# A transformer block on one core: down product in four PSUM banks, weights split in three pieces, SyncE in written order, row transposes in three jobs

## The chip, the cores and the metric

The kernel runs on one core of one Trainium2 chip. The metric is the device time of one execution in microseconds (us). A core has a matrix engine (PE, with its weight loads shown apart as PEld), VectorE (DVE), ScalarE (ACT), GpSimd (POOL) and SyncE (SP), which only issues transfers here. Each engine takes its instructions in one order and waits at the first that is not ready.

## The reference, cut to what matters

```python
x = A_x                                            # 2048 x 576, f32; 32 heads of 18
h  = x + attention(layernorm(x), wqkv) @ wo        # full softmax attention
n  = layernorm(h)
h2 = h + (gelu(n @ w_gate) * (n @ w_up)) @ w_down  # 576 -> 4608 -> 576
```

All tensors are f32 in DRAM. The kernel keeps f32 accuracy on a 16-bit matrix engine by splitting operands into a high and a low f16 part and adding three products.

## The kernel before, in words

**Attention.** The 2048 rows are four blocks of 512. Heads go in groups of four, so that there are 32 steps (group, block), each a loop over 16 key tiles `kt`. For each key tile PE makes the scores of four heads into two-bank tiles `pair0`/`pair1`, ACT exponentiates them (L579), and PE weighs the values into a single bank (`weigh`, L583). VectorE meanwhile takes the row maxima for a later step (`max_unit`, L533), one and a half steps ahead, so that in the last step and a half no maxima are left. What else has to be done in that stretch is dealt out by Python generators: `take(side, 2)` and `take(fill, 2)` advance two helpers by two yields per key tile. `out_block` normalises a finished step and sends it by DMA into the transposed store `XT`. `wo_block(b)` is the output projection of block b (8 groups of 14 matmuls of 288 columns, evicted by VectorE at L688). `pair_rows(0)` makes the rows for the first pair of blocks and transposes them by DMA.

**The gated product.** The 576-wide product with gate and up weights uses a seven-product scheme for 2x2 blocks, over pairs of row blocks p = 0, 1 (`pair_rows(p)` makes the seven row combinations, f16 high and low parts, and transposes them into `X` and `V`). The 4608 columns are 18 chunks of 256. `unit(c, p)` is chunk c of pair p: 14 products of 7 matmuls with 512 columns each, and a gelu, gate and high/low split on ACT and VectorE (`high` L879 on ACT, `low` L882 on VectorE). `down(p)` multiplies two chunks by the down weights: 16 groups of 12 matmuls with 288 columns, each evicted by VectorE (L958). One round of the main loop is two units, a down product, two more units and a down product.

**Weights.** `split_matrix` prepares one weight matrix of a chunk: POOL forms four sums (L787 to L790), `exponents` finds the largest magnitude (VectorE reduces the columns, L125 and L128; PE turns the result by a transpose, L132; VectorE reduces again, L134; PE spreads it over the partitions, L139; VectorE copies it, L141), and ACT and VectorE split the scaled weights (L796, L800, L804) in two pieces. This short chain back and forth between VectorE and PE is called a turn below. `split_down` does the same with the down weights. These run as `side` generators beside the products. All weight tiles are loaded into one buffer, `W8` (inside region `A`), so the next load waits until the last split has read it.

**Banks.** The units use six banks: three singles, both banks of `pair0` and one of `pair1`. The down product and the turns share the two that are left, `bank3` and the second bank of `pair1` (`down_ring = m_ring`). PE, ACT, VectorE and POOL run in the order in which the code is written; SP is ordered by a scheduler except in the first stage.

## Time and profile before

| | us |
|---|---|
| median of 3 runs | 2968.07 |
| lowest, highest | 2966.96, 2974.78 |
| the profiled execution: its own time | 2965.44 |
| its span, first to last instruction | 2963.7 |
| VectorE's maxima (L533), busy | 1264.6 |
| matrix engine, busy | 2697.1 |
| VectorE, busy | 2247.1 |

The profiled execution's own time is 1.74 us more than its span and 2.63 us below the median. A busy matrix engine is not one at its peak: matmul ends are modelled, and the distance from start to start of equal groups says more than the busy share. `PE bank<-W,WK` names the tile written and those read, without buffer numbers. In brackets at the end of a row stands how long the engine was idle before it and what released it. `PEclk` is the clock granted to the matrix engine as a share of full speed.

### The profile page before, as it was taken

How to read it: one execution, taken by the hardware profiler on the slowest of the kernel's cores; microseconds unless marked ns; L12 is line 12 of the kernel's file. 1: busy time of each engine (PE TensorE's matmuls, PEld its weight loads, DVE VectorE, ACT ScalarE, POOL GpSimd, SP SyncE). 2: the span in 40 equal slices, each digit the busy share in tenths (PEclk: the TensorE clock that was granted, in tenths of full speed). 3: DMA queues.
4: the chain of work that ended last, by engine and by line, in shares of the span. 5: the costliest groups of instructions: out<-in, count | busy, mean ns of one | idle time of the engine just before them, and what ended most of it. 6: DMA issues, size and time to landing. Idle time of an engine off the chain costs nothing.

```text
span 2963.7 us, 43958 instructions
## 1 busy us (share of the span) xinstructions
PE 2697.1 (91%) x16755; PEld 1110.7 (37%) x16755; DVE 2247.1 (76%) x4068; ACT 1590.2 (54%) x1826; POOL 524.8 (18%) x683
## 2 busy tenths in 40 slices
PE   7999999999999999999967699999999999999999
PEld 3542222222222222222323345555555555555555
DVE  6369999999999999999775556565656565656563
ACT  4218888888888888888542133333333333333332
POOL 2102421212121211212140211111111111111100
PEclk9999999999999999999988899999999999999999
DMA  7221010101010100100141211010101010101011
GB/s 211 66 68 49 14 36 13 34 14 38 14 37 14 28 18 19 33 16 23 47 96 40 54 42 36 20 36 20 36 20 36 20 36 20 36 20 37 20 50 41
DMA packets 170855, 111.99 MB, mean 38 GB/s; under 512 B 84596, under 2 KB 151924, under 8 KB 170644
## 3 DMA queue, kind: packets, MB, share of 16 engines
q1 hardware_dynamic: 165284, 99.90, 12.4%
q0 software_dynamic: 5360, 9.29, 1.2%
q8 instruction: 131, 2.15, 0.3%
q14 instruction: 80, 0.66, 0.1%
HBM read 74.45 MB, written 14.42 MB: 30 GB/s over the span
## 4 chain that ended last, share of the span: by engine, by line
DVE 55%; PE 35%; ACT 4%; DMA 3%; issue 2%; SPq 1%; POOL 0%; DVEq 0%; ACTq 0%; POOLq 0%
DVE mx L533 39%; PE pair L279 9%; PE bank L279 9%; PE bank L868 8%; PE pair L868 7%; DVE WK L882 2%; DVE ac_m L125 1%; ACT WK L879 1%; DMA A<-in_B_w_down_dram 1%; DVE nat L958 1%; DVE W L844 1%; DVE tmp L876 1%; DVE W L800 1%; PE bank L583 1%; DMA X<-A 1%
## 5 line engine op out<-in xcount | busy, mean ns | idle before, releaser
L533 DVE TENSOR_REDUCE mx<-bank 128x1 f32<-128x512 f32 x2048 | 1264.6, 682 | 25.4 <-PE bank L530 25.3
L579 ACT ACTIVATE WK<-pair,p_ex_sc 128x1024 f32<-128x1024 f32 x1024 | 1084.5, 1113 | 236.7 <-PE pair L577 235.6
L583 PE MATMUL bank<-WK,V 128*32 128x512 f32 x4096 | 548.3, 607 | 0.1
L279 PEld LDWEIGHTS <-WK 128*128 128x128 f16 x3456 | 338.1, 98 | 156.4 <-issue 51.6
L868 PEld LDWEIGHTS <-W 128*128 128x128 f16 (+1 forms) x2394 | 234.2, 98 | 317.0 <-issue 50.0
L530 PE MATMUL bank<-W 54*128 54x512 f16 x1024 | 289.8, 381 | 38.0 <-DVE mx L533 9.4
L530 PE MATMUL bank<-A 54*128 54x512 f16 x1024 | 279.1, 380 | 35.2 <-DVE mx L533 6.5
L279 PE MATMUL bank<-W,WK 128*128 128x288 f16 x1824 | 253.6, 287 | 29.9 <-DVE nat L958 20.3
L279 PE MATMUL pair<-W,WK 128*128 128x288 f16 x1632 | 226.4, 289 | 21.7 <-DVE nat L958 18.3
L583 PEld LDWEIGHTS bank<-WK,V 128*32 128x32 f32 x4096 | 81.2, 108 | 433.3 <-issue 405.3
L868 PE MATMUL pair<-X,W 128*128 128x512 f16 (+1 forms) x792 | 221.6, 384 | 22.2 <-ACT tmp L889 10.3
L868 PE MATMUL pair<-V,W 128*128 128x512 f16 (+1 forms) x720 | 203.1, 380 | 8.5 <-ACT tmp L918 3.0
L606 POOL TENSOR_TENSOR rp<-rc,minus_one 128x16 f32<-128x16 f32 x28 | 81.8, 2923 | 617.3 <-DMA rc<-nat 617.3
L787 POOL TENSOR_TENSOR A<-A 128x384 f32<-128x384 f32 x36 | 36.3, 1007 | 807.6 <-DVE A L804 407.9
L796 ACT ACTIVATE W<-A,p_s_m 128x1152 f16<-128x1152 f32 (+1 forms) x52 | 72.6, 1412 | 198.2 <-DVE p_s_m L171 198.2
L577 PE MATMUL pair<-W 56*128 56x512 f16 x1024 | 158.7, 378 | 6.0 <-ACT WK L579 5.3
L577 PE MATMUL pair<-A 56*128 56x512 f16 x1024 | 156.1, 376 | 1.5 <-ACT WK L579 0.8
L958 DVE SCALAR_TENSOR_TENSOR nat<-bank,p_dsc,nat 128x288 f32<-128x288 f32 x152 | 78.3, 515 | 97.9 <-PE bank L279 95.8
L530 PEld LDWEIGHTS <-W 54*128 54x128 f16 x1024 | 59.0, 93 | 221.1 <-issue 219.3
L530 PEld LDWEIGHTS <-A 54*128 54x128 f16 x1024 | 56.7, 93 | 208.7 <-issue 205.3
L958 DVE SCALAR_TENSOR_TENSOR nat<-pair,p_dsc,nat 128x288 f32<-128x288 f32 x136 | 70.0, 515 | 81.3 <-PE pair L279 80.0
L868 PEld LDWEIGHTS <-A 128*128 128x128 f16 x882 | 86.2, 98 | 108.2 <-DMA X<-A 5.4
(279 smaller groups left out, 2913.2 us busy)
## 6 DMA issues: line engine op xcount, KB each, us to landing
A<-in_B_w_down_dram SPq DMA_DIRECT2D x9, 1152.0 KB
A<-in_B_w_up_dram SPq DMA_DIRECT2D x72, 128.0 KB
A<-in_B_w_gate_dram SPq DMA_DIRECT2D x68, 128.0 KB
nat<-rc SPq DMA_DIRECT2D x32, 256.0 KB
qk_hi<-qk SPq DMA_DIRECT2D x36, 128.0 KB
qk_lo<-qk SPq DMA_DIRECT2D x36, 128.0 KB
A<-in_A_x_dram SPq DMA_DIRECT2D x32, 144.0 KB
out_dram<-nat SPq DMA_DIRECT2D x16, 288.0 KB
```

Of the source, the lines that this page charges most:

```text
L279: nc.tensor.matmul(dst, a, b, start=(i == 0), stop=(i == len(pairs) - 1))
L530: nc.tensor.matmul(pms[j][:, :TB], Q[r, q0 : q0 + P], K[r, kc * TB : (kc + 1) * TB], start=True, stop=True)
L533: nc.vector.tensor_reduce(mx[:, t, 2 * pr + j, kc : kc + 1], pms[j][:, :TB], axis=AX.X, op=ALU.max)
L577: nc.tensor.matmul(pS[:, j, :TB], K[r, kt * P : (kt + 1) * P], Q[r, qc * TB : (qc + 1) * TB], start=True, stop=True)
L579: nc.scalar.activation(pes[(2 * kt + pr) % NPE], pS[:, :, :TB], AF.Exp, scale=ex_sc)
L583: nc.tensor.matmul(acc[32 * hh : 32 * hh + 32, :TB], Vg[n // NB][:, kt * G4 + hh * VC : kt * G4 + hh * VC + 32], pes[(2 * kt + hh // 2) % ...
L606: nc.gpsimd.tensor_tensor(rc, den, minus_one.to_broadcast([P, R]), op=ALU.pow)
L787: nc.gpsimd.tensor_add(W8[:, S1], W8[:, A21], W8[:, A22])
L796: nc.scalar.activation(wh[:, a:b], W8[:, a:b], AF.Copy, scale=s)
L868: nc.tensor.matmul(bank, w, x_, start=start and i == 0, stop=i == len(mm) - 1, skip_group_check=not start)
L882: nc.vector.tensor_sub(hl[:, 2 * i + j], v, hh[:, 2 * i + j])
L958: nc.vector.scalar_tensor_tensor(nat[:, t, ws], pt[:, :HALF], dsc, nat[:, t, ws], op0=ALU.mult, op1=ALU.add)
```

## The change

Eight edits go together.

1. **Banks.** The pair tiles are given up after attention, and four single tiles `more0` to `more3` take their place. The units use three singles and three of these; `down_ring` now has four banks, the two that were left and those of the second product of each unit; the turns keep two.
2. **Turns.** `exponents` yields twice (`space=2`; six times in the attention stretch) between the last reduction and the transpose on PE, and again before the spreading product. The four POOL sums are dealt out one per yield.
3. **Weights in three pieces** (4:7, 0:2, 2:4). The next matrix is loaded as soon as the first piece is split (`then`), or after the third for the down weights; a matrix takes 8 transfers in place of 10.
4. `low` of every unit goes from VectorE to POOL.
5. `pair_rows` has three jobs with three row buffers in place of two with two (for pair 1: one), pair 1's high parts are made by ACT in place of VectorE, and its second transpose of each round is issued by ACT. The last contraction piece is a full 128 rows with zeros in place of 96.
6. **SP in written order** after the attention loop. The last `out_block` issues four of its nine transfers on ACT.
7. `wo_block` loads whole rows of x two ahead, and starts at key tile 11 in place of 9.
8. **The order in the transition.** `take(side, 3)`, the first rows spread over the last step, the second chunk's gate prepared there; the rows of pair 1 run beside `unit(1, 0)` and the first down product; the rounds of the main loop are regrouped so that one unit at a time takes one matrix.

```diff
-    banks = [singles[0], singles[1], singles[2], pairs2[0][:, 0], pairs2[0][:, 1], pairs2[1][:, 0]]
-    down_ring = m_ring = ring([singles[3], pairs2[1][:, 1]])
+    more = [ps2.tile([P, 512], F32, name=f"more{i}") for i in range(4)]
+    banks += singles[:3] + more[:3]
+    m_ring = ring([singles[3], more[3]])
+    down_ring = ring([more[3], singles[3], singles[1], more[1]])
...
         nc.vector.tensor_reduce(am, ac, axis=AX.X, op=ALU.max)
-        yield
+        for _ in range(space):
+            yield
         pt = next(m_ring)
...
-        for a, b in ((4, 7), (0, 4)):
+        for k, (a, b) in enumerate(((4, 7), (0, 2), (2, 4))):
...
+            if k == at and then is not None:
+                then()
...
         def low(i, j, v):
-            nc.vector.tensor_sub(hl[:, 2 * i + j], v, hh[:, 2 * i + j])
+            nc.gpsimd.tensor_sub(hl[:, 2 * i + j], v, hh[:, 2 * i + j])
...
-                    nc.sync.dma_start_transpose(dst, rows[:, (a - k0) * P : (b - k0) * P])
+                    (turn_on[a % 2] if p else nc.sync).dma_start_transpose(dst, flat[:, (a - k0) * P : (b - k0) * P])
...
+    in_order.enter_context(tc.manual_schedule(engines={EngineType.SP}))
...
+    beside(it, side, 1, 1)
+    beside(unit(1, 0), side, 1, 1)
+    while not dscs:
+        take(side)
+    beside(down(0, dscs[-1], NCH == 2), side, 2)
...
+            side = chain(until_ready(g2))
+        beside(unit(c, 1), side)
...
+            side = chain(g2, pause(2), u2, pause(2), g3, pause(2), u3, pause(5), dn)
+        beside(unit(c + 1, 1), side)
+        beside(down(1, dsc, last), side)
```

**A turn inside a down product.** VectorE's order in the second down product of a round, before (`nat<-` is an eviction, `ac_m`, `am_m` and `a_m` the reductions of the turn):

```order
L958 SCALAR_TENSOR_TENSOR nat<-bank_71,p_dsc,nat 128x288
L125 TENSOR_REDUCE ac_m_21825<-A 128x1 x2
L958 SCALAR_TENSOR_TENSOR nat<-pair_67,p_dsc,nat 128x288
L128 TENSOR_REDUCE am_m_21826<-ac_m_21825 128x1
L958 SCALAR_TENSOR_TENSOR nat<-bank_71,p_dsc,nat 128x288
L134 TENSOR_REDUCE a_m_21857<-pair_67 1x1
L136 TENSOR_SCALAR a_m_21857<-a_m_21857 1x1
L141 COPY ab_m_21861<-bank_71 128x1
```

The same place in the changed kernel (L990 is the eviction, L126, L130, L137 and L145 the turn):

```order
L990 SCALAR_TENSOR_TENSOR nat<-more_12743,p_dsc,nat 128x288
L126 TENSOR_REDUCE ac_m_21918<-A 128x1
L130 TENSOR_REDUCE am_m_21919<-ac_m_21918 128x1
L990 SCALAR_TENSOR_TENSOR nat<-more_12745,p_dsc,nat 128x288
L990 SCALAR_TENSOR_TENSOR nat<-bank_69,p_dsc,nat 128x288
L137 TENSOR_REDUCE a_m_21966<-bank_69 1x1
L139 TENSOR_SCALAR a_m_21966<-a_m_21966 1x1
L990 SCALAR_TENSOR_TENSOR nat<-bank_67,p_dsc,nat 128x288
L990 SCALAR_TENSOR_TENSOR nat<-more_12743,p_dsc,nat 128x288
L145 COPY ab_m_21996<-more_12745 128x1
```

Two evictions now lie between each reduction and the next step of the turn, where there was one or none; the evictions go round four banks, and the transpose of the turn is put into `bank_69`, the bank of the eviction just ahead of it.

**The transposes of pair 1.** SP's order before, beside the first down product (one round of the four is the first three rows):

```order
L748 DMA_TRANSPOSE X<-A 128x9x128 x2
L748 DMA_TRANSPOSE V<-A 128x2x128
L748 DMA_TRANSPOSE V<-A 128x15x128
L748 DMA_TRANSPOSE X<-A 128x9x128 x2
L748 DMA_TRANSPOSE V<-A 128x2x128
```

ACT's order there in the changed kernel, with the semaphores that each row waits for (`DMAHW` are transfers issued by SP and ACT, `CAST A<-A`, `V<-A` and `A<-W` the three high parts of a round):

```order
L733 CAST A<-A 128x4x288 [waits DMAHW7_49,DMAHW0_49,Pool_49]
L750 DMA_TRANSPOSE X<-A 128x9x128 [waits DMAHW2_49,DMAHW1_49,DMAHW3_49,DVE_49,Activation_49]
L733 CAST V<-A 128x2x288 [waits Pool_49]
L733 CAST A<-W 128x288
L733 CAST A<-A 128x4x288 [waits DMAHW5_49,DMAHW4_49,Pool_49]
L750 DMA_TRANSPOSE X<-A 128x9x128 [waits DMAHW6_49,DMAHW0_49,DMAHW7_49,DVE_49,Activation_49]
```

One of five transposes of a round is now ACT's, and it stands behind a wait for three transfers (the previous round's last transposes on SP); ACT's second and third high part of the round stand behind it.

237 lines of the change are left out of this document (133 added, 104 removed).

## The prediction

> **What bounds the kernel now.** I read the page for the stages, then the busy time by stretch, then the matrix engine's rows in order of time with the idle time ahead of each. The stretches:
>
> ```profile
> 200.00:1456.00 1256.00, 1182.20 (x8031) 279.73 (x8029) 1237.49 (x2056) 1055.09 (x1026) 281.46 (x408) 1.00 0.10 27
> 1456.00:1578.90 122.90, 85.79 (x579) 36.49 (x576) 70.29 (x154) 54.62 (x57) 38.38 (x41) 0.89 0.36 77
> 1578.90:1650.30 71.40, 53.31 (x266) 27.53 (x266) 45.47 (x108) 19.91 (x29) 5.78 (x7) 0.88 0.15 43
> 1650.30:1706.30 56.00, 30.32 (x183) 20.30 (x183) 30.07 (x59) 1.31 (x2) 16.28 (x23) 0.81 0.37 70
> 1706.30:1783.90 77.60, 72.17 (x398) 39.37 (x399) 45.67 (x90) 22.90 (x33) 13.66 (x14) 0.96 0.15 37
> 1783.90:2963.70 1179.80, 1100.22 (x6328) 616.74 (x6325) 704.56 (x1359) 373.63 (x540) 137.81 (x124) 1.00 0.10 30
> ```
>
> The columns are stretch, length, then busy time of PE, PEld, DVE, ACT, POOL, clock, DMA share, GB/s. Up to 1456 VectorE is busy 1237 of 1256 us with maxima; the change touches nothing there, so I price it at nothing. From 1456 to 1783.9, the transition, nobody is full: PE 70%, 75%, 54%, 93%, at a lowered clock. From 1783.9 on eight rounds of the main loop run, with PE the fullest engine. One round by the starts of its six parts:
>
> ```profile
> 2005.47 1.68 PE L868 MATMUL bank<-X,A 128*128 128x512 f16 x7
> ...
> 2026.68 1.68 PE L868 MATMUL bank<-X,W 128*128 128x512 f16 x7
> ...
> 2036.52 0.27 PE L132 MATMUL bank<-id,am_m 128*1 128x128 f32 x1 [0.59 <-DVE am_m L128]
> ...
> 2049.46 1.27 PE L279 MATMUL bank<-W,WK 128*128 128x288 f16 x9
> ...
> 2055.51 1.63 PE L279 MATMUL bank<-W,WK 128*128 128x288 f16 x12 [1.03 <-DVE nat L958]
> ...
> 2079.99 1.68 PE L868 MATMUL bank<-X,A 128*128 128x512 f16 x7
> ...
> 2093.99 0.38 PE L139 MATMUL pair<-a_m,ones 1*128 1x1 f32 x2
> 2094.30 0.60 PE L868 MATMUL pair<-V,W 128*128 128x512 f16 x2
> ...
> 2102.45 1.68 PE L868 MATMUL bank<-X,W 128*128 128x512 f16 x7
> ...
> 2109.22 1.67 PE L868 MATMUL pair<-X,W 128*128 128x512 f16 x7 [2.06 <-ACT tmp L889]
> ...
> 2128.41 1.63 PE L279 MATMUL bank<-W,WK 128*128 128x288 f16 x12
> ...
> 2152.90 1.68 PE L868 MATMUL bank<-X,A 128*128 128x512 f16 x7
> ```
>
> The parts last 21.21 (a unit without side work), 22.78 (unit), 30.53 (down), 22.46, 25.96 (units) and 24.49 us (down, no side work): 147.43. Four units at 21.21 and two down products at 24.49 would be 133.82. So 13.6 us a round is lost, 6.0 of it in the down product that runs beside splits (from 2049.46) and 4.75 in the last unit (from 2102.45), to waits for VectorE, for evictions, and to false sharing: at 2109.22 PE wants the second bank of a pair tile and waits until ACT has read the first.
>
> **Part by part: the main loop.** Single banks remove the false sharing (2.06 us here). Four banks let PE run four groups, about 5.9 us (4 of 16 x 24.49), ahead of VectorE in place of two; the 1.03 us kind of wait goes. Spaced turns let VectorE finish a reduction some 3 us before PE wants it (two products), where the wait was 0.59. What stays of a turn is the spreading, 0.31 us (2093.99 to 2094.30), and a transpose of about a third of that: 0.4 x 5 turns = 2.0. One turn a round puts its transpose into the bank of the group just issued, so PE still waits for that eviction, about 0.7. What is late next: the last `low` ahead of the down product, now on POOL.
>
> ```profile
> L620 POOL TENSOR_TENSOR nat<-nat x31: 1152/1156/1241, 282.6 to 1520.9; 128x512 f16<-128x512 f32 x31
> ...
> 1830.02 0.69 DVE L882 TENSOR_TENSOR WK<-WK 128x512 f16<-128x512 f32 x1 [0.68 <-ACT WK L879]
> ...
> 1831.78 1.00 POOL L787 TENSOR_TENSOR A<-A 128x384 f32<-128x384 f32 x1 [3.27 <-DMA A<-in_B_w_gate_dram]
> ...
> 1832.06 1.26 DVE L882 TENSOR_TENSOR WK<-W,WK 128x512 f16<-128x512 f32 x1
> ```
>
> POOL has done the same operation at the same size in attention: 1.156 us against 0.69 on VectorE. The down product wants the last of these only at its 12th matmul, 1.5 us of unit and 1.4 us of down product after its source exists, so 0.5 us more hides. Beside a POOL sum the VectorE operation grew from 0.69 to 1.26 us. Sixteen lows a round, at up to 0.57 us each, are 9 us of VectorE lost to neighbours and 11 us (16 x 0.69) given back; nothing on balance, with VectorE at 60% (704.56 of 1179.8).
>
> [...]
>
> A round becomes 133.8 + 2.0 + 0.7, and no more than the unhidden rest: I take 136.5, bounds 134 (turns cost nothing) and 142 (over half the loss stays). Gain 10.9 in each of seven rounds and 5 in the last, which has no side work in its second half: **81** (40 to 99).
>
> Three edits I price at nothing. A third piece of each matrix adds three short instructions on ACT and VectorE; were each as long as a whole 0.69 us operation, that is 4 x 3 x 0.69 = 8 us a round of two engines that are not the bound, under PE's products. SP in written order: behind a load that waits for its buffer stands only the next load, and the pause of two to five products behind each (3 to 7.6 us) covers its flight, if the split that frees the buffer is not late; what that costs where it fails is the last rival. The tail matmul over 128 rows in place of 96 streams as many columns. No row quoted here separates the two; were time to go with rows, 14 of a unit's 98 matmuls would be a third longer, 1.0 us of 21.21, 36 us over 36 units, which I keep for the upper end. It can't gain.
>
> **The transition.** Attention's last 24 key tiles and the chain behind it:
>
> ```profile
> 1471.51 3.54 PE bank L279 x28
> ...
> 1476.58 3.55 PE bank L279 x28
> ...
> 1501.04 0.37 PE L132 MATMUL bank<-id,am_m 128*1 128x128 f32 x1 [10.43 <-DVE am_m L128]
> ...
> 1508.11 0.39 PE L577 MATMUL pair<-W 56*128 56x512 f16 x2 [0.31 <-ACT WK L579]
> 1510.12 0.39 PE L577 MATMUL pair<-W 56*128 56x512 f16 x2 [0.30 <-ACT WK L579]
> ...
> 1524.36 0.77 PE L279 MATMUL bank<-W,X 128*128 128x288 f16 x3 [4.60 <-DMA X<-nat]
> 1533.73 1.60 PE L279 MATMUL bank<-W,X 128*128 128x288 f16 x6 [8.60 <-DMA X<-nat]
> ...
> 1560.54 1.90 DMA rc<-nat
> ...
> 1574.48 0.70 SPq L635 DMA_DIRECT2D X<-nat  x1
> 1575.22 0.70 SPq L636 DMA_DIRECT2D X<-nat  x1
> ```
>
> A key tile alone takes 2.01 us, one with two groups of `wo_block` 5.07: 16 x 2.01 + 8 x 5.07 = 73 us, where 1456 to the first transfer of the chain at 1560.54 is 104.5. Three waits make 23.6 of the 31.5 between. The first goes by spacing, the others because `wo_block` starts two key tiles later and SP's transposes are spread. But VectorE carries 70 us up to 1578.9 and gets more (a second chunk's reductions, the normalising of a step that POOL did), so I take 87.5: gain **17** (3 to 28). Behind it nine transfers at 0.74 us each become five, ACT issuing four beside them: gain **3** (0 if the landing decides, 3 if the issue does).
>
> The output projection of the last block and the rest of the first two units take 71.4 us (1578.9 to 1650.3). Needed are 8 x 1.77 (3.54 is two groups) and 20 products at 1.515 (21.21/14) = 44.5, and three turns. Waits that go:
>
> ```profile
> 1586.82 4.06 DMA A<-in_A_x_dram
> ...
> 1619.12 0.37 PE L132 MATMUL bank<-id,am_m 128*1 128x128 f32 x1 [8.48 <-DVE am_m L128]
> ...
> 1660.28 1.35 SPq L748
> 1661.68 3.32 DMA X<-A
> ...
> 1666.41 3.04 PE L279 MATMUL pair<-W,WK 128*128 128x288 f16 x12 [6.75 <-DVE nat L958]
> ...
> 1667.46 4.14 DMA V<-A
> ...
> 1674.52 1.30 SPq L748
> ```
>
> I take 50: gain **21** (12 to 26). The very first down product lasts 56 us (1650.3 to 1706.3), since rounds of pair 1's rows follow each other every 14.24 us (1660.28 to 1674.52) through one buffer, and evictions queue behind them on VectorE. Three buffers shorten a round, but ACT's transpose waits for SP's last three, and SP's next for ACT's: 3.32 on ACT, then three issues of 1.3 and a last landing of about 3.4 on SP, 10.6 us a round, estimated. Four rounds are 42 us; they begin some 10 us before the down product. It ends with them, at 32: gain **24** (10 if rounds stay at 14.24, 32 if all hides). Behind ACT's transpose stand only the row parts there; behind VectorE's work on those parts stand evictions, which four banks cover for 5.9 us.
>
> [...]
>
> The three parts to 1783.9 (77.6 us) become 21.2 + 22.2 + 24.9 and about 1 us for the weights that can be loaded only after the last transpose: gain **8**. The sum: 17 + 3 + 21 + 24 + 8 = 73 in the transition, 81 in the loop, **154**. 2965.4 - 154 = 2811, and since that execution is 2.6 us below the median, I say **2812**.
>
> **The rivals.** A measurement of this kernel tells about 0.3%, 9 us, from no change.
>
> *The transition stays* (0.16). VectorE is the hidden bound of attention's end, and the rows of pair 1 hold the down product as before. For it: 70 us of VectorE in a stretch of 104.5, and ACT, SP and VectorE waiting for each other's transposes. Against it: the three waits on PE are each for one late item, not for a full engine. Then only 3 + 12 + 8 of 73 come: 2965 - 23 - 81 = 2861.
>
> *The loop stays* (0.11). Waits move instead of going: a matrix loads after one piece, POOL's sums and VectorE's reduction wait for it at the head of their queues. Say 3 us a round are left of the 10.9: 2965 - 73 - 24 = 2868. Against it: VectorE is at 60% over the loop, so cover is missing, not capacity. Both together (0.04): 2918.
>
> *Slower* (0.09). POOL takes its lows in order behind sums that wait for a load.
>
> ```profile
> POOL A L787 <- DMA A<-in_B_w_gate_dram: 94.7, 13, 16.6
> ```
>
> Such a wait is 7.3 us on average, 16.6 at most. If it stands in front of a low at each of the 18 down products, PE waits it out: at 16.6 that is +299, 3110 us. It decides from (154 + 9)/18 = 9.1 us each. Against it: in the written order the sums for the next matrix stand behind the lows of the unit before a down product.
>
> *No change* (0.03): the edits cancel. That the change doesn't do what it says holds only for the turn in the shared bank, priced above.
>
> **How the numbers follow.** The forecast has 0.57, its own range 2775 to 2850. The range of 2772 to 2875 adds the two partial cases, and leaves out the double failure, no change, the slower case and a little of the best. Faster: 0.57 + 0.16 + 0.11 + 0.04 = 0.88; no change 0.03; slower 0.09.
>
> **What would show it.** Right: rounds of about 136.5 us; no wait of a `pair` kind by ACT copies; the down product beside splits below 26 us; the very first down product, beside the rows of pair 1, near 32; the attention stretch below 90. Wrong: PE idle released by POOL's lows at the start of down products; idle PE behind evictions that wait for ACT's transposes; rounds above 142.

## The result, and the profile after

The changed kernel takes 2885.93 us (median of 4 runs, 2882.49 to 2889.06) against 2970.85 for the kernel before: a ratio of 0.9714, with a 95% interval of 0.9693 to 0.9735. The forecast was 2812, in a range of 2772 to 2875. The direction was right, and just over half of the gain came: 85 us of 154. The profiled execution has a span of 2881.6 us, 82.1 less than before.

In the page of the changed kernel, the busy time of each engine:

```profile
PE 2678.4 (93%) x16755; PEld 1115.0 (39%) x16755; DVE 2180.2 (76%) x3995; ACT 1606.3 (56%) x1872; POOL 685.3 (24%) x833
```

The work moved as the diff says: POOL has 685 us where it had 525, VectorE 67 us less. That says nothing yet on where the time went. For that I cut both executions at the same five events: the transfer of the sums of steps 31 and 32 (`rc<-nat`), the first matmul of the very first down product, the start of `unit(0, 1)`, and the start of the loop's next round. In SP's and PE's rows of the kernel before (the second event, 1560.54, is in the prediction's last-step rows):

```profile
1488.17 0.61 SPq L600 DMA_DIRECT2D rc<-nat  x1
...
1648.88 1.27 PE L279 MATMUL bank<-W,WK 128*128 128x288 f16 x9
1706.33 1.03 PE L868 MATMUL bank<-X,A 128*128 128x512 f16 x2 [5.09 <-DMA X<-A]
1783.78 1.46 PE L868 MATMUL bank<-X,A 128*128 128x512 f16 x6
```

The same five in the changed kernel, then the parts of one later round:

```profile
1486.26 0.65 SPq L603 DMA_DIRECT2D rc<-nat  x1
1557.87 0.63 SPq L603 DMA_DIRECT2D rc<-nat  x1
...
1641.02 1.51 PE L282 MATMUL more<-W,WK 128*128 128x288 f16 x11
1677.80 1.67 PE L900 MATMUL bank<-X,A 128*128 128x512 f16 x7
1758.02 1.67 PE L900 MATMUL bank<-X,A 128*128 128x512 f16 x7
...
1898.25 1.46 PE L900 MATMUL bank<-X,A 128*128 128x512 f16 x6
1941.71 1.63 PE L282 MATMUL more<-W,WK 128*128 128x288 f16 x12
1965.23 1.67 PE L900 MATMUL bank<-X,A 128*128 128x512 f16 x7
2009.68 1.51 PE L282 MATMUL more<-W,WK 128*128 128x288 f16 x11
2038.33 1.67 PE L900 MATMUL bank<-X,A 128*128 128x512 f16 x7
```

| stretch | before | after | gain | forecast |
|---|---|---|---|---|
| up to the sums of step 31 | 1488.2 | 1486.3 | 1.9 | 0 |
| attention's last step | 72.4 | 71.6 | 0.8 | 17 |
| its chain, output projection, rest of two units | 88.3 | 83.2 | 5.2 | 24 |
| very first down product | 57.4 | 36.8 | 20.7 | 24 |
| two units and a down product, to the loop | 77.5 | 80.2 | -2.8 | 8 |
| the loop, eight rounds | 1179.9 | 1123.6 | 56.3 | 81 |

The first line is not told from nothing: in the kernels of the experiments, which share the code up to there, the same event lies between 1483.7 and 1492.4 us. The forecast counted attention's end from 1456 on, so at most these 1.9 us belong to its 17 as well.

A round lasts 140.1 us (1898.25 to 2038.33) where 136.5 was forecast: two units 43.5, a down product without splits 23.5, two units 44.5, a down product beside splits 28.7. The profile lists four waits of PE in that round:

```profile
2001.60 0.27 PE L135 MATMUL bank<-id,am_m 128*1 128x128 f32 x1 [0.93 <-DVE am_m L130]
2018.66 1.63 PE L282 MATMUL more<-W,WK 128*128 128x288 f16 x12 [2.94 <-DVE nat L990]
2022.69 0.27 PE L135 MATMUL bank<-id,am_m 128*1 128x128 f32 x1 [0.93 <-DVE nat L990]
2026.57 1.63 PE L282 MATMUL more<-W,WK 128*128 128x288 f16 x12 [0.36 <-DVE ab_m L145]
```

Three of the four lie in the down product, and the largest is a wait for an eviction with four banks at hand. The order in time of ACT, then of VectorE, ahead of that eviction tells why (L829 is ACT's part of a weight piece, L832 and L834 VectorE's, L911 `high`, L908 the gate, L990 the eviction):

```profile
2015.17 0.62 ACT L911 CAST WK<-WK 128x512 f16<-128x512 f32 x1 [2.82 <-DVE WK L908]
2015.70 0.93 ACT L829 ACTIVATE W<-A,p_s_m 128x768 f16<-128x768 f32 x1
...
2012.39 0.75 DVE L832 SCALAR_TENSOR_TENSOR WK<-A,p_s_m,W 128x512 f16<-128x512 f32 x1 [1.61 <-ACT W L829]
...
2016.66 0.90 DVE L832 SCALAR_TENSOR_TENSOR WK<-A,p_s_m,W 128x512 f16<-128x512 f32 x1 [1.52 <-ACT W L829]
2018.09 0.52 DVE L990 SCALAR_TENSOR_TENSOR nat<-more,p_dsc,nat 128x288 f32<-128x288 f32 x1
```

The last two pieces of the up weights (`u2`) fall on the last two products of the unit. ACT comes to the third piece only behind a `high` that waits 2.82 us for a gate; VectorE waits 1.52 us for that piece, and the first eviction stands behind it and its tail. The down product began at 2009.68, and with four banks full PE stood from 2015.72.

### The profile page after: what moved, and what is told of

It is laid out like the page before. It is cut to its first block, busy times and chain, and to the rows that moved or that the text cites. A ratio compares the mean times of both kernels' runs of the same rounds, so it can differ in the third digit from the quotient of the medians.

```text
span 2881.6 us, 43910 instructions
## 1 busy us (share of the span) xinstructions
PE 2678.4 (93%) x16755; PEld 1115.0 (39%) x16755; DVE 2180.2 (76%) x3995; ACT 1606.3 (56%) x1872; POOL 685.3 (24%) x833
## 3 DMA queue, kind: packets, MB, share of 16 engines
q1 hardware_dynamic: 150479, 95.30, 12.3%
q10 hardware_dynamic: 4837, 1.25, 0.2%
## 4 chain that ended last, share of the span: by engine, by line
DVE 46%; PE 41%; DMA 4%; ACT 2%; issue 2%; SPq 2%; POOL 1%; ACTq 0%; DVEq 0%; POOLq 0%
DVE mx L536 39%; PE more L900 11%; PE bank L900 10%; PE bank L282 8%; PE more L282 6%; PE pair L282 3%; DMA A<-in_B_w_up_dram 1%; SPq L798 1%; DMA A<-in_B_w_gate_dram 1%; DMA nat<-rc 1%; PE bank L533 1%; DVE ac_m L126 1%; PE bank L586 1%; DVE W L834 1%; DVE nat L990 1%
## 5 line engine op out<-in xcount | busy, mean ns | idle before, releaser
L900 PEld LDWEIGHTS <-W 128*128 128x128 f16 x2394 | 233.3, 98 | 280.6 <-issue 10.5
L282 PE MATMUL more<-W,WK 128*128 128x288 f16 x1728 | 233.1, 289 | 33.2 <-DVE nat L990 26.8
L282 PE MATMUL bank<-W,WK 128*128 128x288 f16 x1728 | 229.3, 290 | 4.0 <-DVE nat L990 4.0
L900 PE MATMUL more<-X,W 128*128 128x512 f16 x792 | 224.0, 379 | 0.0
L900 PE MATMUL more<-V,W 128*128 128x512 f16 x720 | 203.8, 381 | 0.0
L810 POOL TENSOR_TENSOR A<-A 128x384 f32<-128x384 f32 x144 | 144.1, 1021 | 162.6 <-DMA A<-in_B_w_up_dram 130.9
L914 POOL TENSOR_TENSOR WK<-tmp,WK 128x512 f16<-128x512 f32 x73 | 88.4, 1211 | 390.7 <-ACT WK L911 340.4
L918 ACT COPY tmp<-bank 128x512 f32<-128x512 f32 x36 | 21.0, 583 | 273.0 <-PE bank L900 273.0
L990 DVE SCALAR_TENSOR_TENSOR nat<-bank,p_dsc,nat 128x288 f32<-128x288 f32 x144 | 73.6, 516 | 87.2 <-PE bank L282 85.9
L829 ACT ACTIVATE W<-A,p_s_m 128x768 f16<-128x768 f32 (+1 forms) x78 | 79.1, 1037 | 103.5 <-DVE p_s_m L174 102.9
```

Source lines behind the costliest of these rows:

```text
L282: nc.tensor.matmul(dst, a, b, start=(i == 0), stop=(i == len(pairs) - 1))
L810: op(W8[:, d], W8[:, a], W8[:, b])
L829: nc.scalar.activation(wh[:, a:b], W8[:, a:b], AF.Copy, scale=s)
L900: nc.tensor.matmul(bank, w, x_, start=start and i == 0, stop=i == len(mm) - 1, skip_group_check=not start)
L914: nc.gpsimd.tensor_sub(hl[:, 2 * i + j], v, hh[:, 2 * i + j])
L990: nc.vector.scalar_tensor_tensor(nat[:, t, ws], pt[:, :HALF], dsc, nat[:, t, ws], op0=ALU.mult, op1=ALU.add)
```

## The experiments

Each kernel is the changed one with the edit shown; under "Together" several edits are put on top of one another. Medians in us stand beside the ratio to the kernel before on the same chip, with its interval; what a kernel is worth against the changed one is its ratio less 0.9714, times 2968.

**Four parts of the change undone, one each.**

```diff
-            nc.gpsimd.tensor_sub(hl[:, 2 * i + j], v, hh[:, 2 * i + j])
+            nc.vector.tensor_sub(hl[:, 2 * i + j], v, hh[:, 2 * i + j])
```

> The changed kernel (2886 us) with the low part of every unit back on VectorE; nothing else differs. Theory A (the prediction's: low costs nothing on either engine, 11 us of VectorE a round given back are balanced by what the neighbours lose to POOL): 2878 to 2894, rounds of 140. Theory B (VectorE's queue in front of the down product is what PE waits for; the low that stands there now is one more item of 0.7 us, twice a round, and the waits of 2.94 us grow): 2898 to 2912, rounds near 142. Theory C (POOL's lows block VectorE's two-input operations): faster, 2850 to 2875, and VectorE's operations of 128x512 beside units get shorter.

2877.32, 0.9698 (0.9683 to 0.9712): 5 less in the medians, with overlapping intervals, so not told apart. Rounds stay at 140.4 (two rounds together 280.8), PE's wait for an eviction is 2.00 us in place of 2.94, and a wait of 0.64 for the down weights' reduction is new. In the loop PE's listed waits make 33.8 us for 36.6. In front of the first down product PE no longer waits 3.44 us for POOL. Theory A, 0.7 us below its range, for as long as other things are late; the last group comes back to it.

```diff
-    down_ring = ring([more[3], singles[3], singles[1], more[1]])
+    down_ring = m_ring
```

> The changed kernel with the down product in two banks, those of the turns, as in the kernel before; the units keep six single banks. Theory A (four banks hide lateness of evictions): the down product beside splits grows from 28.7 to about 31, that without splits stays near 23.5 to 24.5, the very first one grows by 5 to 10 since evictions there stand behind waits for ACT; 2886 + 8 x 3 + 8 = 2918 (2905 to 2930). Theory B (four banks only move the wait, since VectorE is late at the start of the product, when no bank is taken yet): 2886 to 2895.

2918.83, 0.9837 (0.9821 to 0.9854): 36 more, theory A. The down product beside splits takes 35.1 us for 28.7, and PE's wait in it is

```profile
2026.78 3.04 PE L282 MATMUL bank<-W,WK 128*128 128x288 f16 x12 [6.59 <-DVE nat L990]
```

in place of 2.94: two groups more or less of lead are 3 us, and the late pieces are there with either. The rest of the 6.4 us is speed: behind this wait two groups take 3.04 and 3.08 us in place of 1.63, and from their starts to the next group's (2026.78, 2029.61, 2032.49) it is 2.83 and 2.88 us, where the changed kernel has 1.46 behind its wait (2018.66 to 2020.12). Four banks are worth more than I took them for.

```diff
-    def exponents(views, name, space=2):
+    def exponents(views, name, space=1):
```

(and the same for `split_matrix`)

> The changed kernel with one yield in place of two (six stay six in attention) between the steps of a turn; the loads and pieces that follow move up by two yields a turn as well. Theory A (spacing hides a reduction of 1 us and the second one of 0.4): about 0.6 us more a turn, five a round, so 3 us a round and 24 in all: 2910 (2900 to 2920). Theory B (the waits left in the loop are set by when the weights land and by pieces late on ACT): the waits move with the pieces, 2880 to 2895.

2895.88, 0.9759 (0.9744 to 0.9773): 13 more, between the theories.

```diff
-        for k, (a, b) in enumerate(((4, 7), (0, 2), (2, 4))):
+        for k, (a, b) in enumerate(((4, 7), (0, 4))):
```

(and the down weights are loaded after the second piece, which is now the last)

> The changed kernel with the matrices split in two pieces (4:7, 0:4) in place of three, the next load still after the first piece. Theory A (the prediction's: three pieces cost and bring nothing): 2878 to 2894. Theory B (the last pieces that stand on VectorE in front of the down product make PE's wait of 2.94 us there; in two pieces the last of them comes one yield earlier, but is longer): 2870 to 2880 if the earlier end decides, 2894 to 2905 if a longer piece on ACT delays the unit's own copies.

2895.07, 0.9759 (0.9745 to 0.9774): 13 more, which neither theory had for that reason. In both kernels everything behind a matrix's first piece comes one or two products earlier, and so does the turn that needs the next load. PE's rows, first of the one yield, then of two pieces:

```profile
2000.71 0.37 PE L135 MATMUL bank<-id,am_m 128*1 128x128 f32 x1 [2.75 <-DVE am_m L130]
```

```profile
2003.85 0.27 PE L135 MATMUL bank<-id,am_m 128*1 128x128 f32 x1 [2.30 <-DVE am_m L130]
```

These are the wait of 0.93 us at 2001.60 above, grown: the third piece and the second yield work as time for the load to land, and two yields of pause do not cover it. That is not all of the 13 us. The wait of 2.94 is gone from both kernels, but in both PE now waits 1.1 us a round for POOL's last `low` at the head of the down product, and 0.7 to 1.6 us at the turns that follow it. PE's listed waits in the loop make 45.7 us with one yield and 45.2 with two pieces, for 36.6 in the changed kernel. With two pieces:

```profile
2017.87 0.30 PE L282 MATMUL more<-W,WK 128*128 128x288 f16 x1 [1.13 <-POOL WK L914]
```

**The pause.**

```diff
-            side = chain(g2, pause(2), u2, pause(2), g3, pause(2), u3, pause(5), dn)
+            side = chain(g2, pause(6), u2, pause(2), g3, pause(2), u3, pause(5), dn)
```

> The changed kernel with six yields in place of two between the pieces of g2 and the turn of u2, so that the turn comes four products later and the last two pieces of u2 fall into the down product, after its first evictions. Theory A (PE's 2.94 us wait in the down product is VectorE standing at u2's pieces, which ACT makes late since its third piece stands behind a high part that waits for a gate; and the 0.93 us ahead of the turn is the load's flight): both waits go, rounds from 140.1 to about 136.5, 7 rounds, 25 us: 2858 (2850 to 2868). Theory B (work of VectorE and ACT beside the products is merely moved and comes up in front of later evictions): 2880 to 2892, rounds of 139 to 141.

2853.62, 0.9612 (0.9597 to 0.9626): 30 less, theory A. One changed number gives the forecast's round, 136.96 us between these:

```profile
1759.00 1.24 PE L900 MATMUL bank<-X,A 128*128 128x512 f16 x5
...
1895.96 1.24 PE L900 MATMUL bank<-X,A 128*128 128x512 f16 x5
```

The waits of 2.94 and of 0.93 for the load are both gone; what is left are 1.04, 0.61 and 0.36 us a round at banks that turns and evictions share. The edit moves the pieces and lengthens the load's cover at once, so two more kernels take one of these each.

```diff
-            side = chain(g2, pause(2), u2, pause(2), g3, pause(2), u3, pause(5), dn)
+            side = chain(g2, pause(2), until_ready(u2), pause(4), u2, pause(2), g3, pause(2), u3, pause(5), dn)
```

> The changed kernel with the turn of u2 where it was, and four yields between the end of that turn and the pieces of u2, so that only the pieces move into the down product, not the turn. Theory A (pieces in front of the first eviction make the 2.94 us, and most of the 30 us that six yields ahead of the turn brought): rounds of 137 to 138, the 0.93 us ahead of the turn stays: 2864 (2858 to 2870). Theory B (it was the load's cover): 2878 to 2890. Theory C (pieces later also load the next matrix later, and its turn waits in the down product): 2866 to 2878, with a new wait for a reduction there.

2854.1, 0.9614 (0.9598 to 0.963): all of the 30, by the pieces alone; theory A, and more than it said. Rounds are 136.7 to 137.0, and the turn still waits 0.72 us for its load.

```diff
-                eng.dma_start(W8[: 3 * KR, b + a, 2], tail[:, a].unsqueeze(0).to_broadcast(
-                    [3, KR, P]))
+            for r in range(3):
+                eng.dma_start(W8[r * KR : (r + 1) * KR, b : b + 2, 2], tail)
```

> The changed kernel with the tails of a matrix loaded by six transfers of 32 rows, as before the change, in place of four that spread 32 rows over three groups of partitions. Theory A (the load lands late because of these four: SP needs 0.73 to 0.8 us for each, and in the last 2 us of a load the DMA engines show 60 to 66 GB/s at two tenths busy, after up to 276 GB/s): the load lands 1 to 2 us earlier, the 0.93 us in a round and part of the 5.02 us ahead of the loop go: 2876 (2870 to 2880). Theory B (issue and flight together are no shorter with ten transfers): 2881 to 2890.

2885.86, 0.9722 (0.9706 to 0.9738): nothing, theory B's time, though A's mechanism is there. VectorE's reduction no longer waits for the load, and PE no longer for the reduction; the down product takes it all back. PE's first wait in the round:

```profile
2015.37 3.04 PE L282 MATMUL more<-W,WK 128*128 128x288 f16 x12 [3.58 <-DVE nat L990]
```

So in the changed kernel the late load cost nothing by itself: whatever PE gained ahead of the down product it lost at the pieces, 3.58 us for 2.94, and in the group behind them, which takes 3.04 us for 1.63. The rounds are 141.0 and 142.1 us.

**Banks for the turns.**

```diff
-    down_ring = ring([more[3], singles[3], singles[1], more[1]])
+    down_ring = ring([banks[0], banks[3], banks[1], banks[4]])
```

> The changed kernel with the down product in four banks of the units (the first and second product's of gate and up), so that the turns have their two banks for themselves. Theory A (a turn's transpose in the bank of an eviction just ahead costs PE 0.93 us, and a product in the turn's bank 0.36): 1.3 us a round, 10 in all: 2876 (2870 to 2881). Theory B (the wait is VectorE's lateness, and PE meets it at the next product if not at the turn): 2882 to 2890. Theory C: the units' first and second banks come free later than the turns' banks, and the start of the down product pays: 2890 to 2900.

2882.8, 0.9706 (0.9692 to 0.9721): no measurable change, theory B's time. The 0.93 at the shared bank and the 0.36 are gone from PE's rows, the 2.94 is not, and the round stays at 140.1. Where the 1.3 us went, PE's row behind that wait shows:

```profile
2015.47 3.00 PE L282 MATMUL bank<-W,WK 128*128 128x288 f16 x12 [2.94 <-DVE nat L990]
```

The group takes 3.00 us in place of 1.63, and the next one starts 2.83 us after it, at 2018.30; behind the same wait in the changed kernel that distance is 1.46 (2018.66 to 2020.12), at a granted clock of 1.00. Over the loop PE's listed waits fall from 36.6 to 27.5 us, but behind this wait all seven groups are slow here (2.2 to 3.0 us), and three of seven in the changed kernel. So what a wait less brings was in part paid back in speed. Why groups are slow in one round and not in another these runs do not show. With the late pieces moved this is different, see below.

**The transposes of pair 1, and the rows of pair 0.**

```diff
-    turn_on = (nc.sync, nc.scalar)
+    turn_on = (nc.sync, nc.sync)
```

> The changed kernel with all five transposes of a round of pair 1 on SP. Theory A (ACT's transpose and SP's four wait for each other, 10.4 us a round, and ACT's in-order queue holds up VectorE's row parts and so the evictions): rounds of 5 x 1.3 = 6.6 us if SP is the limit, the very first down product from 47 to 32 to 36, and the 4.18 us wait of a unit for ACT behind its transpose goes: 2868 to 2876. Theory B (the rounds are held by the chain of POOL, ACT, VectorE and the row buffers, not by who issues): 2882 to 2890. Theory C (one queue is the slower, as five issues in a row are longer than four beside one): 2892 to 2900.

2876.65, 0.9693 (0.9676 to 0.9709): 6 less in the medians, with overlapping intervals, nearest to theory A; in the profile the first down product lasts 31.7 us (36.8 with ACT), and what lies ahead of it 74.2 (83.2). Two transposes of ACT in the changed kernel, with the first and the last of SP's four between them, then SP's waits from 1640 to 1690 (us in all, times, longest):

```profile
1659.54 1.30 ACTq L750 DMA_TRANSPOSE X<-A  x1
...
1662.92 1.30 SPq L750 DMA_TRANSPOSE X<-A  x1
...
1667.08 1.32 SPq L750 DMA_TRANSPOSE V<-A  x1
...
1669.96 1.30 ACTq L750 DMA_TRANSPOSE X<-A  x1
```

```profile
SPq L750 <- DMA X<-A: 13.7, 3, 5.7
```

SP starts 3.4 us after ACT, when ACT's transpose has landed, and ACT again 2.9 us after SP's last: 10.42 us in this round, where 10.6 was estimated. The two rounds before it took longer, 17.0 and 12.3 us (ACT's transposes at 1630.25, 1647.21 and 1659.54); in the second of them ACT also waited 4.73 us for POOL's combinations. No run here has transposes on two queues without these waits for each other, so what a round would take without them is not shown. On SP alone rounds come every 8.4 to 11.4 us, not 6.6, so something other than its issues holds them then; which of POOL, ACT, VectorE and the buffers was not tried apart.

```diff
             for (o0, o1, f), r in zip(jobs, parts):
-                high(r[:, :, :HALF], f)
+                full = p or i == 0
+                if full:
+                    high(r[:, :, :HALF], f)
```

(and the three VectorE operations behind it under the same condition)

> The changed kernel without the high and low row parts of three of the four rounds of pair 0 (the values are those of the first round again; normalising, row combinations and transposes all stay). Theory A (at attention's end VectorE is full in a stretch of 65 us, and PE's turns and weighing stand behind its row work, 8.24 + 1.68 + 8.29 us): the output projection of the last block begins 10 to 15 us earlier: 2872 to 2877. Theory B (what holds attention's end is the queue of transposes and of context transfers on SP): less than 4: 2882 to 2888.

2880.9, 0.97 (0.9682 to 0.9718): not told from the changed kernel by the times. In the profile the last step lasts 64.1 us (71.6). PE's waits, first of the changed kernel, then of this one:

```profile
1500.96 0.37 PE L135 MATMUL bank<-id,am_m 128*1 128x128 f32 x1 [8.24 <-DVE am_m L130]
...
1526.16 0.41 PE L282 MATMUL bank<-W,X 128*128 128x288 f16 x2 [1.96 <-DMA X<-nat]
1539.93 0.37 PE L135 MATMUL bank<-id,am_m 128*1 128x128 f32 x1 [8.29 <-DVE nat L696]
```

```profile
1503.30 0.37 PE L135 MATMUL bank<-id,am_m 128*1 128x128 f32 x1 [8.25 <-DVE am_m L130]
1527.80 0.90 PE L282 MATMUL bank<-W,X 128*128 128x288 f16 x3 [5.52 <-DMA X<-nat]
```

The 8.29 went with the rows (theory A), and 3.6 us of it came back as a longer wait for the context's transfers, which stand behind transposes on SP (theory B's). The first 8.25 stays because the first round's work was left in.

```diff
-                take(rows, 3)
+                take(rows, 2)
```

> The changed kernel with the rows of pair 0 dealt out at two yields a key tile in place of three, so that they last through the whole last step. Theory A (VectorE is full only where row work is dealt densely, and PE's 8.24 and 8.29 us stand behind it): less of it comes in front of each turn, both waits shrink to 4 to 6: 2878 (2874 to 2882). Theory B (the order of a round and the turn decides, not the density; rows that end later also put their transposes in front of the last context's transfers on SP): 2884 to 2894.

2874.28, 0.9683 (0.9668 to 0.9697): 9 less, theory A. With all the work in, the last step takes 62.2 us, and the two long waits are halved:

```profile
1497.29 0.27 PE L135 MATMUL bank<-id,am_m 128*1 128x128 f32 x1 [3.79 <-DVE am_m L130]
...
1532.35 0.37 PE L135 MATMUL bank<-id,am_m 128*1 128x128 f32 x1 [4.27 <-DVE nat L696]
```

So VectorE is not too small for that stretch; a round of rows was dealt as one lump in front of a reduction of 1.8 us. The lump is also slow: ahead of the wait of 8.24 the changed kernel has eight row operations (1490.54 to 1498.92) that take 8.7 us beside POOL's combinations and sums. The same eight of a later round (1517.63 to 1525.03) take 4.0, while POOL issues loads or stands. How much of the 9 us is less work in front and how much fewer slowed operations was not tried apart.

```diff
-                             pause(10), until_ready(second))
+                             pause(10))
```

> The changed kernel with the turn of the second chunk's gate no longer in attention's last step but beside the first unit, its load where it was. Theory A (attention's end is full: its reductions, its four POOL sums beside VectorE's rows and PE's 8.29 us there are the price of doing more in this step): the output projection of the last block begins 4 to 9 us earlier, but the steps of pair 1 and the down weights come 8 yields later and the first down product starts with less of them done, 3 to 8 back: 2880 to 2888 in all. Theory B (the wait there is VectorE behind rows, whatever PE asks for; the eviction of the output projection meets it instead): the projection begins at the same time within 2 us, and the time is 2888 to 2896.

2896.41, 0.9756 (0.974 to 0.9772): 12 more. (So much comes later here that `unit(1, 0)` takes some up weights before they are split.) The last step is 3.7 us shorter, and the first down product lasts 53.7 us, with PE waiting 15.34 us for pair 1's transposes at its end: theory A in kind, but more is given back than it said, and the time is 0.4 us above B's range. That product ends with its rows here, not with its matmuls.

**Together.**

```diff
# six yields ahead of u2's turn, the down product in the units' banks,
# all transposes on SP, and
-            side = chain(until_ready(g2))
+            side = chain(pause(0 if sc else 5), until_ready(g2))
```

> The changed kernel with four edits together: the turn of u2 six yields after the pieces of g2, the down product in the units' banks, all transposes of pair 1 on SP, and in the first round of the main loop the turn of the third chunk's gate five products later. Theory A (each takes away a wait of its own): rounds of 135 to 135.5 (137.0 with the first edit alone, less 0.6 + 0.4 + 1.0), 8 times 1.8 from there and 6 for the transposes, and 4.7 for the turn that PE waits for in front of the loop: 2854 - 14 - 6 - 5 = 2829 (2820 to 2838). Theory B (with one wait gone PE meets the next late item): 2842 to 2854.

2819.52, 0.95 (0.9486 to 0.9514): 64 less, theory A. Rounds are 134.7 and 134.9 us (1736.84 to 1871.50 to 2006.40), 2.2 less than with the pause alone, whose waits of 1.04, 0.61 and 0.36 us are gone: the turns' own banks now pay. The loop has one listed wait of PE left, 0.2 us.

The same with `low` on VectorE:

> The same four edits, with low back on VectorE. Theory A (low on POOL costs only where POOL also makes row combinations, 3.4 to 4.4 us ahead of the first down product, and nothing in the loop): 4 us less than with four edits: 2825 (2816 to 2834). Theory B (with VectorE's queue less full of late pieces in front of the down product, its own lows there now stand in the way): 5 to 12 more than with four edits.

2834.84, 0.9553 (0.9538 to 0.9567): 15 more than with four. Theory A is wrong, and B sized too small. `low` on VectorE costs 1.9 us a round (136.6, from 1741.35 to 1877.92), and PE waits for VectorE's reduction:

```profile
1868.58 0.27 PE L135 MATMUL bank<-id,am_m 128*1 128x128 f32 x1 [1.87 <-DVE am_m L130]
```

`low` on POOL was worth nothing that could be measured while late pieces kept VectorE waiting, and 15 us once they did not.

The four edits, `low` on POOL, and `take(rows, 2)`:

> The four edits (turn of u2 later, down product in the units' banks, transposes of pair 1 on SP, first turn of the loop later), low on POOL, and the rows of pair 0 at two yields a key tile. Theory A (attention's last step and the rest lose time each for itself): 2819.5 less the 8.7 that two yields brought alone: 2811 (2805 to 2817). Theory B (the gain of the denser last step comes back as a wait behind it): 2817 to 2824.

2809.65, 0.9469 (0.9453 to 0.9485): 10 less than the four, theory A: the forecast's time, 2812, by five small edits. SP's and PE's rows at the same five events as above:

```profile
1485.62 0.65 SPq L603 DMA_DIRECT2D rc<-nat  x1
...
1547.64 0.63 SPq L603 DMA_DIRECT2D rc<-nat  x1
...
1623.06 1.51 PE L282 MATMUL bank<-W,WK 128*128 128x288 f16 x11
1654.82 1.46 PE L900 MATMUL bank<-X,A 128*128 128x512 f16 x6
1722.59 1.67 PE L900 MATMUL bank<-X,A 128*128 128x512 f16 x7
```

The gains of the table's lines from the second on are now 10.4, 12.9, 25.7, 9.7 and, with a span of 2803.1, 99.4. That the sum meets the forecast is luck in part: the loop gives 18 us more than was forecast, and attention's end and its chain give 18 less.

The last three build on these five.

```diff
-    beside(islice(it, 2), side)
+    run(islice(it, 2))
```

> The same five, and no side work beside the first two products after attention, so that VectorE's reciprocal of the last step stands ahead of the first pieces of the second chunk, and their next load starts later. Theory A (the last step's chain takes 17.5 us to its transfers where it took 13.9, since the reciprocal waits 3 us behind those pieces and the broadcast of reciprocals flies beside a weight load, 6.1 us for 4.9): 3 to 5 less than the five: 2807 (2803 to 2809). Theory B (the pieces are then late in front of the next unit, and the output projection is not what the transition ends with): 2809 to 2816.

2806.74, 0.9466 (0.9449 to 0.9484): theory A's time, but not told from the five. The edit does what it should: from `rc<-nat` to the first context transfer 12.7 us for 17.1. But the first down product takes 34.1 for 31.8, with waits of 2.87 and 2.44 us for evictions, and from the last sums to its end the profile has 108.6 us for 107.2.

```diff
-            nc.gpsimd.tensor_sub(hl[:, 2 * i + j], v, hh[:, 2 * i + j])
+            eng = nc.vector if (c, p) == (1, 0) else nc.gpsimd
+            eng.tensor_sub(hl[:, 2 * i + j], v, hh[:, 2 * i + j])
```

> The same five, with the lows of the unit ahead of the very first down product on VectorE. Theory A (PE waits 4.4 us there for POOL, which has four row combinations in front of its last low): 3 to 4 less than the five: 2808 (2805 to 2810). Theory B (VectorE is then late with rows of pair 1 and with evictions by the same): 2809 to 2814.

2809.12, 0.9469 (0.9451 to 0.9487): no measurable change, theory B. PE's row in the five, then here:

```profile
1629.02 0.30 PE L282 MATMUL bank<-W,WK 128*128 128x288 f16 x1 [4.44 <-POOL WK L914]
```

```profile
1647.12 3.04 PE L282 MATMUL bank<-W,WK 128*128 128x288 f16 x12 [2.75 <-DVE nat L991]
```

The wait of 4.44 for POOL is gone, and waits for evictions behind rows stand in its place, the longest of 2.75; the product lasts 33.1 us.

Both edits on top of the five:

> The five with both. Theory A: 6 to 8 less than the five: 2804 (2800 to 2807). Theory B (the first down product ends with its rows and their transposes, whatever starts earlier): 2807 to 2815.

2805.66, 0.9454 (0.944 to 0.9469): 4 less than the five, with overlapping intervals, so the times do not decide between the theories. In the profile the stretch from the last sums to the end of the first down product is 106.9 us for 107.2, which speaks for B. It has the lowest median of all these kernels, 5.5% below the kernel before.

## Why the prediction was wrong

**The main loop, 81 forecast, 56 measured.** Banks and spacing did what was said: waits for a pair tile by ACT copies are gone, the down product without splits went from 24.5 to 23.5, and undoing four banks or spacing costs 36 and 13 us. The step that failed is "what is late next: the last `low` ahead of the down product, now on POOL". No wait of PE for POOL is listed in the changed kernel's whole loop (with one yield, or with two pieces, there is one, 1.1 us a round). Late next were the last pieces of the matrix that the units before had just begun to split, in front of the first eviction (2.94 us a round). With them failed the sentence that a pause of two to five products covers a load: two did not cover it (0.93 us), and did with the transfers of before (4.8 us of issue and no wait). Whether its condition held, that the split which frees the buffer is not late, is open: with either set of transfers VectorE waited 2.33 us for ACT's part of that piece. Moving the last pieces removes 30 us, and only then do the turns' own banks count. The forecast's bound of 134 for a round, where turns cost nothing, is nearly what the better kernels reach (134.7). The shared bank was priced right at 0.7 (0.93 measured), yet in the changed kernel its removal brings nothing. A term that the forecast lacks is the matrix engine's speed behind a wait: behind the wait for the pieces three of seven groups took 2.6 to 3.0 us for 1.63 (the slowest, at 2301.42, at a granted clock of 0.50), and two of the groups next to them 2.4 and 2.9, which makes 5.7 us in the loop.

**Low on POOL** was priced at nothing on balance. In the changed kernel that holds (5 us in the medians the other way, not told apart); with VectorE on time it is 15 us to the good, 1.9 a round. Beside a `low` in the changed kernel's loop VectorE's gates (L908, 0.75 us) and evictions (L990, 0.52) were as long as elsewhere; 15 weight pieces of 128x512 (L832) took 0.90 to 1.20 us, the others 0.75. At attention's end more was slow. VectorE's row parts, two of a round beside POOL's combinations, and the same two of a later round, when POOL only issued loads:

```profile
1506.08 0.88 DVE L736 TENSOR_TENSOR V<-V 128x128 f16<-128x128 f32 x1
1506.89 0.78 DVE L737 COPY V<-V 128x128 f16<-128x128 f16 x1
...
1519.56 0.28 DVE L736 TENSOR_TENSOR V<-V 128x128 f16<-128x128 f32 x1
1519.77 0.21 DVE L737 COPY V<-V 128x128 f16<-128x128 f16 x1
```

**Three pieces** were priced at nothing, and undoing them costs 13 us, by the load's cover and by the waits that came with it.

**Attention's last step, 17 forecast, 0.8 measured.** "The first goes by spacing" failed: 10.43 us became 8.24. What decides is not the turn's own length but what VectorE has in front of the reduction, and the change put a round of pair 0's rows there. The other two waits did go or shrink (8.60 to none, 4.60 to 1.96), and a new one for VectorE, 8.29, took their place. That VectorE gets more to do in this stretch was seen (84.4 us from 1456 to 1578.9, where it was 70.3); that it comes in lumps, and slowed beside POOL, was not. Two yields in place of three give 9 us of the 17.

**The chain, the output projection and the rest of two units, 24 forecast, 5 measured.** The chain was to gain 3 and lost 4.8: from `rc<-nat` to the last group that waits for the context 23.2 us (1557.87 to 1581.10) in place of 18.4. In the changed kernel, VectorE's and SP's rows:

```profile
1560.52 1.02 DVE L832 SCALAR_TENSOR_TENSOR W<-A,p_s_m,W 128x768 f16<-128x768 f32 x1 [0.32 <-ACT W L829]
...
1563.48 0.25 DVE L614 RECIPROCAL rc<-rc 128x16 f32<-128x16 f32 x1
...
1575.36 0.74 SPq L636 DMA_DIRECT2D X<-nat  x1
```

The reciprocal stands behind two pieces of the second chunk, the side work that the change brought here. Only the transfers at the end were costed, not what was put in front of the reciprocal. With nothing put there the first context transfer leaves 12.7 us after the sums, in place of 17.1, so the step is shown. It was 9.9 before the change (1560.54 to 1570.44); what the other 2.8 are was not tried. The time did not follow measurably, because of the next point. Of the other 21 came 10. Of the 11 that are missing 4.18 were lost to ACT, whose transpose waits in front of a unit's copy (1.3 us with transposes on SP), 1.5 in the group behind that wait, which takes 3.14 us for 1.67 at a granted clock of 0.50, and 2.33 and 1.35 in waits for VectorE.

**The very first down product, 24 forecast, 20.7 measured, and the 8 behind it, -2.8 measured.** The round of 10.6 us came out once (10.42); the two before it took 17.0 and 12.3, and with SP alone the product lasts the 32 us that were forecast. Missed was what comes behind: "about 1 us" for the weights that can be loaded only after the last transpose. Their issue took 5.8 us (1678.89 to 1684.7), their flight and a reduction came behind, and PE stood:

```profile
1689.03 0.37 PE L135 MATMUL bank<-id,am_m 128*1 128x128 f32 x1 [5.02 <-DVE am_m L130]
```

Another 5.5 us of the 80.2 are waits of the loop's kind (1.23, 2.94, 0.94 and 0.37). With four edits, a turn five products later among them, none of these is left, and the stretch takes 67.6 us. What is saved ahead of the first down product is largely given back in it: in the last three kernels PE's wait of 4.44 us for POOL is gone or 0.54, and the product lasts 34.1, 33.1 and 32.4 us for 31.8, with new waits for evictions, which stand behind row parts on VectorE.

**The rivals.** In size the transition came out as the first rival had it (23 forecast for that case, 26 measured), on top of a loop that gave 56. Its cause, VectorE as the bound of attention's end, did not hold: the same work in another order gives 9 us, and with five edits 59 of the 73 come. The second rival had waits move in place of going, so that 3 of the 10.9 us a round would come; waits did move, one as it said (a reduction that waits for a load), but 7.3 came. The slower rival's mechanism, POOL's lows behind other POOL work, is there at one place, 3.44 us ahead of the first down product.

## What to carry to other kernels

In a tuned kernel whose engines run in written order, a wait is priced by what stands ahead of the late item on its engine after the change, and every step that is moved needs that question at its new place: here pieces ahead of evictions, rows ahead of a reduction, a piece ahead of a reciprocal. Removing one wait shows the next, so gains are neither nothing nor sums until they are tried together: separate turn banks and lows on POOL were worth nothing measurable alone and 2 us a round each behind the right pause. Where a stretch ends with a serial chain, such as rows and their transposes, time saved ahead of it can come back as waits in it.

## What was not expected of the hardware

A load's four transfers that spread 32 rows over three groups of partitions took 0.73 to 0.82 us each to issue on SP, beside 0.37 to 0.45 for most of the plain ones, and landed late: VectorE waited 1.35 us at 2000.40 for a load issued up to 1997.6, and not at all with six plain transfers in their place. The DMA view of 1990 to 2003 shows 61 to 66 GB/s at two tenths of the 16 DMA engines at its end. In pair 1's rounds of the changed kernel a transpose of 2 tiles took SP 1.17 to 1.25 us to issue, one of 9 tiles 1.30 to 1.34 and one of 10 tiles 1.34 to 1.36; of those with 5 tiles three took 1.29 to 1.33 and one 2.14. VectorE's 128x128 copy took 0.21 us while POOL only issued loads and 0.78 beside POOL's combinations, almost four times, where the 128x1024 subtraction went only from 1.23 to 1.71. Behind some of PE's waits in the changed kernel the granted clock was 0.50: from 2301.42 to 2304.25, behind a wait of 3.71 us, 12 matmuls took 3.04 us for 1.63, and from 1632.29 to 1635.23, behind one of 4.18, a unit's seven took 3.14 for 1.67. Behind a wait of 2.94 us the group at 2018.66 took 1.63, at a clock of 1.00. Groups of 12 were as slow at 2015.47 with the turns' own banks (3.00 us) and at 2026.78 with two banks (3.04, and 3.08 behind it).
